# Four x tiles ahead of the K weights, four transposes on TensorE, a new order of phase 1

## Chip, cores, metric

One core of a Trainium2 chip. The metric is the device time of one execution in microseconds (us), the median over several executions. The profile's span is shorter than that time, by 1.60 to 1.80 us in the runs with the order of before (1.39 in the one with tiny transfers) and by 1.21 to 1.55 us in those with the new order; where the rest is spent is not shown. Positions below are in us from the start of the span. PE is TensorE and PEld its weight loads, DVE is VectorE, ACT ScalarE, POOL GpSimd, SP SyncE. A landing below, the end of a transfer, is the start of its issue plus the trace's time to landing, good to some 0.05 us.

## The reference

x is layer-normalized once. One branch is linear attention with 32 heads of 16, the other a gated feed-forward; both are added to x.

```python
xn = layernorm(x)                              # x: (1, 2048, 512), bf16
q, k, v = split(xn @ wqkv)                     # wqkv: (512, 1536)
pq, pk = phi(q), phi(k)                        # phi(t) = where(t > 0, t + 1, exp(t)) + 1e-6
kv, z = pk^T v per head, sum of pk
attn = ((pq kv) / (pq z + 1e-6)) @ wo
ffn = (silu(xn @ w_gate) * (xn @ w_up)) @ w_down   # 512 -> 1792 -> 512
out = x + attn + ffn
```

## The kernel before

The 2048 rows are 16 tiles of 128. Phase 1 makes, for each tile: statistics, normalization, the transposed tile, K and Q projections (four matmuls of 512 columns each), phi of both, and an accumulation of four matmuls over pk. That is 16 x 12 = 192 matmuls. Phase 2 is gate, up, down and the attention output. Programs for all engines are recorded in one list, and waits follow from what reads and writes what.

The loads stand at the head, on the SP and ACT issuers (`xhalf` is half a tile, `wpart(e, i, h)` the h-th 256 rows of the K weights, i = 1, or of the Q weights, i = 0):

```python
        xhalf("sp", 0, 0)
        xhalf("act", 0, 1)
        xload("sp", 1)
        wpart("act", 1, 0)
        wpart("sp", 1, 1)
        xload("act", 2)
        wpart("act", 0, 0)
        xload("sp", 3)
        wpart("sp", 0, 1)
        for t in range(4, 16):
            xload("sp", t)
```

Tiles 0 and 1 are only centred before their projection; their scale goes into phi. The projections rotate through four PSUM banks, which three other engines have to empty:

```python
        def nextbank():
            ring[0] += 1
            return 4 + (ring[0] - 1) % 4

        def proj(col, i, t, halves=(0, 1)):
            if 0 in halves:
                at[i, t] = nextbank()
            b = at[i, t]
            src = xcT if t in CENTRED else xnT
            for h in halves:
                K.add("pe", [(lambda e, c=c: e.matmul(
                    banks[b][:, :], src[:, c, t * P:(t + 1) * P], wqkv[:, c, col:col + D],
                    start=(c == 0), stop=(c == NDC - 1))) for c in (2 * h, 2 * h + 1)],
                    r=([("xcT", t, h)] if t in CENTRED else xkeys(t)) + [("wqkv", i, h)], w=[B(b)])

        def rest(t):
            return (1,) if t in CENTRED else (0, 1)
```

ACT takes the exponential of a bank, POOL clips it, the DVE adds the linear part from the bank and so frees it. The order of phase 1 is a text; each word is a step and a tile:

```python
        # S statistics (DVE)   R log and power (ACT)   L, P, A normalization on DVE, POOL, ACT
        # M, C centring of tile 1   a, b centring of tile 0   c, d, W, X transposes on TensorE
        # e, v, Y evacuation on ACT   f, g, w, Z evacuation on DVE   D transpose by DMA
        # K first half of a K projection, k the rest; Q, q the same for Q
        # x, m, s phi of K on ACT, POOL, DVE   y, n, u phi of Q   z keeps a Q for later
        # G accumulation over pk   J scaled tile for G (POOL)   F filler matmuls
        # r, o, N small factors per row that these steps need
        run("""
            S0 R0 b0 a0 d0 S1 M1 c0 F4 r0 C1 R1 g0 J0 W1 f0 K0 S2 r1 v1 k0 o1 S3 J1 R2 K1 x0 k1 L2 Q1 o0 x1 S4
            X2 m0 Q0 Y2 q1 m1 s0 R3 q0 R4 k2 L3 y1 s1 D3 P4 G0 S8 x2 ...   (cut)
        """)
```

## Time and profile before

| | before |
|---|---|
| time, first three executions | 212.65 us (212.52 to 213.04) |
| span of the profiled execution | 211.8 us |
| TensorE busy | 208.0 us, 98% |
| first K matmul | 5.91 us |
| first gate matmul, the start of phase 2 | 48.91 us |

Two positions matter in what follows: the start of phase 2, and in the changed kernel the start of the 13th projection matmul (the first Q matmul of tile 3). Matmul durations in a timeline overlap; work is counted in slots of 0.216 us, and what the starts show beyond that is waiting. The prediction shows how the stages are read.

### The profile page before, as it was taken

What the parts mean: (1) busy time and instruction counts of PE and PEld (TensorE: products, weight loads), DVE (VectorE), ACT (ScalarE), POOL (GpSimd) and SP (SyncE); (2) the same over time, 40 slices, a digit from 0 to 9 for tenths busy, and PEclk for the clock granted to TensorE, in tenths of its full rate; (3) what the DMA queues carried; (4) which work ended last, traced back from release to release, by engine and by line L of the source; (5) the groups of instructions that cost most, each with busy time, mean ns of one, the idle gap of its engine ahead of it and who ended that gap; (6) DMA issues with size and microseconds to landing.
All of it is one profiled execution on the core that took longest, in us unless ns stands there. A gap on an engine that the chain in (4) does not pass through costs nothing.

```text
span 211.8 us, 2736 instructions
## 1 busy us (share of the span) xinstructions
PE 208.0 (98%) x1009; PEld 95.7 (45%) x1009; DVE 129.2 (61%) x224; ACT 70.3 (33%) x146; POOL 62.9 (30%) x92
## 2 busy tenths in 40 slices
PE   8899899999999999999999999999999999999996
PEld 2344344444544444444444444444444444444455
DVE  3898988973864788654654775564639463542122
ACT  4989886406364333122131313021223122130000
POOL 3879877899402322210201220220204000000000
PEclk9999999999999999999999999999999999999999
DMA  6954731399920021102101011101011101100101
GB/s 177 353 139 101 72 73 35 63 387 370 357 88 0 3 50 25 50 0 53 25 25 25 25 29 50 25 25 50 8 44 26 50 7 46 25 25 0 49 25 53
DMA packets 27997, 16.04 MB, mean 76 GB/s; under 512 B 17872, under 2 KB 27984, under 8 KB 27984
## 3 DMA queue, kind: packets, MB, share of 16 engines
q1 hardware_dynamic: 27152, 15.15, 26.3%
q10 hardware_dynamic: 832, 0.72, 1.1%
q8 instruction: 8, 0.13, 0.3%
q14 instruction: 5, 0.04, 0.1%
HBM read 9.70 MB, written 2.10 MB: 56 GB/s over the span
## 4 chain that ended last, share of the span: by engine, by line
PE 90%; DVE 4%; DMA 3%; POOL 1%; SPq 1%; ACT 1%; issue 0%
PE pb L520 46%; PE pb L608 23%; PE pb L389 7%; PE pb L604 7%; PE pb L438 6%; DMA x_sb<-in_A_x_dram 3%; DVE pk L428 1%; SPq L178 1%; DVE pq L428 1%; DVE stats L256 1%; POOL ef L417 1%; ACT ef L410 1%; PE pb L545 0%; PE pb L598 0%; POOL xn L344 0%
## 5 line engine op out<-in xcount | busy, mean ns | idle before, releaser
L528 ACT ACTIVATE sil<-pb 128x512 bf16<-128x512 f32 x56 | 33.3, 597 | 101.2 <-PE pb L520 98.8
L533 DVE TENSOR_TENSOR hT<-pb,sil 128x512 bf16<-128x512 f32 x56 | 38.1, 687 | 36.7 <-PE pb L520 33.8
L520 PE MATMUL pb<-xnT,wg 128*128 128x512 bf16 x224 | 57.8, 379 | 0.0
L520 PE MATMUL pb<-xnT,wu 128*128 128x512 bf16 x224 | 57.8, 379 | 0.0
L608 PE MATMUL pb<-wd,hT 128*128 128x512 bf16 (+2 forms) x252 | 51.4, 355 | 0.0
L570 POOL TENSOR_TENSOR pz<-pq,zbc 128x512 f32<-128x512 bf16 x16 | 18.6, 1163 | 90.5 <-DVE den L575 78.5
L608 PEld LDWEIGHTS pb<-wd,hT 128*128 128x128 bf16 x252 | 23.5, 98 | 25.0
L520 PEld LDWEIGHTS pb<-xnT,wu 128*128 128x128 bf16 x224 | 21.9, 98 | 25.9 <-DVE hT L533 0.2
L520 PEld LDWEIGHTS pb<-xnT,wg 128*128 128x128 bf16 x224 | 21.9, 98 | 25.8
L614 DVE TENSOR_TENSOR out_sb<-pb,x_sb 128x512 bf16<-128x512 f32 (+2 forms) x18 | 11.4, 632 | 33.2 <-PE pb L608 33.2
L389 PE MATMUL pb<-wqkv,xnT 128*128 128x512 bf16 x112 | 25.2, 379 | 0.8 <-DVE pq L428 0.6
L587 DVE TENSOR_TENSOR pq<-pq,rden 128x512 bf16<-128x512 bf16 x16 | 17.5, 1094 | 0.6
L389 PEld LDWEIGHTS pb<-wqkv,xnT 128*128 128x128 bf16 x112 | 10.8, 98 | 14.5 <-DVE pq L428 1.4
L417 POOL TENSOR_SCALAR ef<-ef 128x512 bf16<-128x512 bf16 x25 | 15.8, 634 | 5.0 <-ACT ef L410 4.5
L604 PE MATMUL pb<-M,pk 128*128 128x512 bf16 (+2 forms) x72 | 16.8, 355 | 0.0
L410 ACT ACTIVATE ef<-pb 128x512 bf16<-128x512 f32 x25 | 14.7, 591 | 3.8 <-PE pb L389 3.8
L256 DVE BATCH_NORM_STATS2 stats<-x_sb 128x6 f32<-128x512 bf16 x16 | 10.9, 679 | 3.6 <-DMA x_sb<-in_A_x_dram 3.6
L438 PE MATMUL pb<-pk,xn 128*128 128x512 bf16 x56 | 12.7, 379 | 0.0
L575 DVE TENSOR_REDUCE den<-pz 128x32 f32<-128x512 f32 x16 | 10.8, 675 | 0.0
L428 DVE SCALAR_TENSOR_TENSOR pk<-pb,ef 128x512 bf16<-128x512 f32 x14 | 9.6, 685 | 1.8 <-POOL ef L417 1.6
L461 POOL TENSOR_TENSOR zacc<-zacc,pk 128x512 f32<-128x512 f32 x8 | 10.2, 1279 | 0.6
L604 PEld LDWEIGHTS pb<-M,pk 128*128 128x128 bf16 x72 | 6.8, 98 | 7.4
(77 smaller groups left out, 109.8 us busy)
## 6 DMA issues: line engine op xcount, KB each, us to landing
out_dram<-out_sb SPq DMA_DIRECT2D x15, 128.0 KB, 1.7
x_sb<-in_A_x_dram SPq DMA_DIRECT2D x14, 128.0 KB, 4.5
wg<-in_B_w_gate_dram SPq DMA_DIRECT2D x2, 896.0 KB, 8.3
wu<-in_B_w_up_dram SPq DMA_DIRECT2D x2, 896.0 KB, 9.7
wd<-in_B_w_down_dram SPq DMA_DIRECT2D x2, 896.0 KB, 13.9
wqkv<-in_A_wqkv_dram ACTq DMA_DIRECT2D x2, 256.0 KB, 4.7
wqkv<-in_A_wqkv_dram SPq DMA_DIRECT2D x2, 256.0 KB, 5.0
wqkv<-in_A_wqkv_dram SPq DMA_DIRECT2D x1, 512.0 KB, 7.8
```

Of the source, the lines that this page charges most:

```text
L389: K.add("pe", [(lambda e, c=c: e.matmul(banks[b][:, :], src[:, c, t * P:(t + 1) * P], wqkv[:, c, col:col + D], start=(c == 0), stop=(c == ...
L410: K.add("act", lambda e: e.activation(buf, banks[b][:, :], ACT.Exp), r=[B(b)], w=[bkey])
L417: K.add("pool", lambda e: e.tensor_scalar(out=buf, in0=buf, scalar1=top, scalar2=0.0, op0=ALU.min, op1=ALU.max), r=[bkey] + tkeys, w=[bkey])
L428: K.add("dve", lambda e: e.scalar_tensor_tensor(out=dst, in0=val, scalar=low, in1=mid, op0=ALU.max, op1=ALU.add), r=keys + lkeys, w=[dkey])
L438: K.add("pe", [(lambda e, c=c: e.matmul(banks[c][:, :], src[:, t, c * P:(c + 1) * P], pk[:, t, :], start=first, stop=last)) for c in range ...
L520: fns.append(lambda e, c=c, b=b, w_=w_: e.matmul(banks[b][:, :], w_[:, c, fc * P:(fc + 1) * P], xnT[:, c, C * 512:(C + 1) * 512], start=(c ...
L528: K.add("act", lambda e: e.activation(sil[:, j % 2, :], banks[gb(j)][:, :], ACT.Silu), r=[B(gb(j))], w=[("sil", j % 2)])
L533: K.add("dve", lambda e: e.tensor_tensor(out=hT[:, C % 2, fc, :], in0=banks[gb(j) + 1][:, :], in1=sil[:, j % 2, :], op=ALU.mult), r=[B(gb( ...
L570: K.add("pool", lambda e: e.tensor_tensor(out=pz[:, t % 2, :], in0=pq[:, t, :], in1=zbc[:, :], op=ALU.mult), r=[("pq", t), ("zbc",)], w=[( ...
L587: K.add("dve", lambda e: e.tensor_tensor(out=heads(pq[:, t, :]), in0=heads(pq[:, t, :]), in1=rden[:, i, :][:, :, None].broadcast_to([P, NH ...
L604: fns = [(lambda e, g=g: e.matmul(banks[bank][:, 0:hi - lo], pk[:, t, g * P:(g + 1) * P], M[:, g, lo:hi], start=(g == 0), stop=False)) for ...
L608: fns = [(lambda e, fc=fc: e.matmul(banks[bank][:, 0:hi - lo], hT[:, C % 2, fc, jj * P:(jj + 1) * P], wd[:, fc, lo:hi], start=False, stop= ...
```

## The change

Intent: have four tiles of x early, transpose them on TensorE instead of waiting for a DMA transpose, and order phase 1 so that TensorE does not wait. The loads of tiles 2 and 3 move ahead of the K weights. Tile 3 is transposed on TensorE too. `rest` lets a projection of tiles 0 to 3 run in two halves. The whole order text is new; its start is shown.

```diff
+SPLIT = (0, 1, 2, 3)
         xload("sp", 1)
+        xload("act", 2)
+        xload("sp", 3)
         wpart("act", 1, 0)
         wpart("sp", 1, 1)
-        xload("act", 2)
         wpart("act", 0, 0)
-        xload("sp", 3)
         wpart("sp", 0, 1)
         def rest(t):
-            return (1,) if t in CENTRED else (0, 1)
+            return (1,) if t in SPLIT else (0, 1)
         run("""
-            S0 R0 b0 a0 d0 S1 M1 c0 F4 r0 C1 R1 g0 J0 W1 f0 K0 S2 r1 v1 k0 o1 S3 J1 R2 K1 x0 k1 L2 Q1 o0 x1 S4
-            X2 m0 Q0 Y2 q1 m1 s0 R3 q0 R4 k2 L3 y1 s1 D3 P4 G0 S8 x2 ...   (cut)
+            S0 M1 a0 b0 c0 R0 d0 F2 C1 S3 e0 N0 W1 r0 K0 o0 f0 R3 w1 S2 K1 P3 k0 S1 R2 J0 W3 x0 k1 Q1 L2 R1 w3
+            m0 X2 q1 r1 Z2 Q3 s0 x1 o1 q3 S5 y1 K3 m1 k3 R5 n1 s1 G0 ...   (cut)
         """)
```

More of the change, by code (lines that the diff above doesn't have):

```diff
@@ L487, in bass_parallel_sum__linear_attn_block__swiglu_ffn__prompt_kernel @@
         run("""
-            S0 R0 b0 a0 d0 S1 M1 c0 F4 r0 C1 R1 g0 J0 W1 f0 K0 S2 r1 v1 k0 o1 S3 J1 R2 K1 x0 k1 L2 Q1 o0 x1 S4
-            X2 m0 Q0 Y2 q1 m1 s0 R3 q0 R4 k2 L3 y1 s1 D3 P4 G0 S8 x2 z1 m2 D4 q2 S12 R8 z0 s2 G1 P8 y0 S14 G2
-            P1 D8 y2 S15 z2 q3 n2 R12 S5 D1 k3 P12 y3 S9 R14 q4 n3 D12 x3 L14 R9 k4 u3 m3 R5 D14 N9 s3 y4 q8
-            P5 x4 S10 k8 n4 z8 D5 A9 m4 u4 G3 n1 x8 s4 D9 k12 R15 S13 m8 y8 q14 P15 x12 s8 R13 S11 q12 m12 D15
-            y14 k14 s12 n14 y12 R10 u14 n12 k5 x14 L13 R11 u12 q9 m14 D13 x5 N11 s14 k9 m5 y9 L10 A11 n8 s5
-            k15 D10 n9 S7 x9 q5 z9 m9 D11 S6 R7 G12 n0 x15 s9 R6 q13 m15 y5 L7 s15 D7 q15 n5 y13 L6 u5 n13 q10
-            y15 D6 u13 n15 k10 y10 u15 n10 k11 x10 u10 m10 k13 x11 s10 m11 k7 x13 s11 m13 k6 x7 s13 m7 q7 x6
-            s7 m6 q6 y7 L0 u8 D0 n7 q11 y6 s6 n6 G13 u7 y11 u6 n11 G5 u11 G14 u9 G11 u2 u1 G8 u0 G15 G7 G9 G10
-            G4 G6
+            S0 M1 a0 b0 c0 R0 d0 F2 C1 S3 e0 N0 W1 r0 K0 o0 f0 R3 w1 S2 K1 P3 k0 S1 R2 J0 W3 x0 k1 Q1 L2 R1 w3
+            m0 X2 q1 r1 Z2 Q3 s0 x1 o1 q3 S5 y1 K3 m1 k3 R5 n1 s1 G0 z1 L5 J1 x3 S9 K2 D5 Q0 z3 m3 S4 k2 R9 q0
+            y3 P9 s3 G1 x2 S8 R4 m2 D9 Q2 z0 q2 P4 s2 R8 k5 z2 L8 n3 D4 S15 q5 x5 y0 S12 m5 G2 D8 y5 s5 q9 y2
+            n5 S10 R15 k9 n0 y9 u5 R12 n9 k4 x9 L15 u9 D15 q4 m9 x4 L12 R10 s9 m4 q8 y4 D12 S11 P10 k8 z8 s4
+            n4 R11 D10 G9 S13 x8 N11 A11 G5 m8 u4 y8 n2 s8 D11 G3 R13 S14 A0 P13 k15 S7 R14 k12 n8 D13 x15 L14
+            S6 m15 q10 x12 D14 s15 m12 k11 y10 s12 n10 k10 D0 x11 u10 R7 m11 q15 x10 s11 q11 m10 y15 L7 R6 s10
+            D7 n15 k13 y11 u15 q13 n11 x13 L6 u11 D6 m13 q14 y13 s13 n13 q12 y14 u13 n14 k14 y12 u14 n12 q7
+            x14 u12 m14 k7 y7 L1 s14 D1 n7 k6 x7 u0 m7 q6 u7 x6 s7 m6 G4 y6 s6 n6 G12 u2 G14 u6 u1 G6 u8 G10
+            u3 G11 G15 G8 G13 G7
         """)
```

## The prediction

> **What bounds the kernel now.** I read the page first, for the share of each engine and the chain that ended last, then the table by stage, then TensorE's timeline up to 30 us, then TensorE's and the DVE's waits.
>
> ```profile
> PE 208.0 (98%) x1009; PEld 95.7 (45%) x1009; DVE 129.2 (61%) x224; ACT 70.3 (33%) x146; POOL 62.9 (30%) x92
> PE 90%; DVE 4%; DMA 3%; POOL 1%; SPq 1%; ACT 1%; issue 0%
> ```
>
> TensorE is the bound; 90% of the chain that ended last is its own work. The stages, cut where its work changes (columns: stretch, its length, busy time of each engine, clock, DMA share, GB/s):
>
> ```profile
> 0.00:5.91 5.91, 4.72 (x20) 1.79 (x21) 2.67 (x9) 3.05 (x11) 2.31 (x13) 1.00 0.66 194
> 5.91:10.18 4.27, 4.02 (x24) 1.42 (x21) 3.67 (x10) 4.01 (x15) 3.71 (x10) 1.00 1.09 356
> 10.18:25.60 15.42, 14.85 (x68) 6.60 (x69) 14.36 (x32) 14.07 (x38) 12.91 (x25) 1.00 0.61 111
> 25.60:39.41 13.81, 13.81 (x64) 6.22 (x65) 11.83 (x22) 10.13 (x21) 10.41 (x17) 1.00 0.23 48
> 39.41:48.91 9.50, 9.50 (x46) 4.31 (x45) 7.06 (x8) 0.60 (x1) 8.95 (x10) 1.00 0.93 297
> 48.91:211.80 162.89, 161.07 (x794) 75.38 (x792) 89.62 (x147) 38.46 (x64) 24.61 (x21) 1.00 0.18 50
> ```
>
> The reader should see that after 25.6 us TensorE never waits again, so only what happens before that can move the end. From 10 to 25.6 us DVE, ACT and POOL are nearly full too: they empty the PSUM banks that the projections need. TensorE's timeline (start, duration, work, wait):
>
> ```profile
> 5.68 0.40 PE L356 MATMUL pb<-ident,hT 128*128 128x128 bf16 x4 [0.33 <-DVE hT L298]
> 5.91 2.55 PE L389 MATMUL pb<-wqkv,hT 128*128 128x512 bf16 x10
> 8.30 0.39 PE L356 MATMUL pb<-ident,xn 128*128 128x128 bf16 x4
> 8.53 1.46 PE L389 MATMUL pb<-wqkv,hT 128*128 128x512 bf16 x6
> 10.18 1.04 PE L389 MATMUL pb<-wqkv,xnT 128*128 128x512 bf16 x4 [0.19 <-DVE pk L428]
> 20.55 4.48 PE L389 MATMUL pb<-wqkv,xnT 128*128 128x512 bf16 x20
> 25.60 3.61 PE L389 MATMUL pb<-wqkv,xnT 128*128 128x512 bf16 x16 [0.57 <-DVE pq L428]
> ```
>
> Durations overlap, so I count in slots. The 44 matmuls that begin at 29.91 start in 9.50 us: 0.216 us each; four transposes take 8.53 - 8.30 = 0.23. Phase 1 has 192 matmuls of 512 columns (41.45 us) and, from 5.91 on, one group of four transposes (0.23). It lasts 48.91 - 5.91 = 43.00 us, so waits take 43.00 - 41.68 = 1.32 us. Slot by slot they are 0.23 us in the first ten matmuls, 0.36 before 10.18 and 0.73 before 25.60. What they waited for:
>
> ```profile
> PEld pb L389 <- DVE pq L428: 1.4, 3, 1.0
> PEld pb L389 <- DVE pk L428: 0.9, 2, 0.7
> PEld pb L389 <- DMA wqkv<-in_A_wqkv_dram: 0.5, 1, 0.5
> DVE stats L256 <- DMA x_sb<-in_A_x_dram: 3.6, 3, 3.1
> ```
>
> The two later waits are for the DVE to free a bank; the first falls on a weight transfer. So the prize is small: no more than 1.3 us of waits, plus whatever earlier start the loads allow.
>
> **What the skill says.** "Perfetto Trace Analysis", Identifying the Most-Contended Engine, warns that matmul busy time does not tell the distance to the roofline. This trace agrees: 98% busy still holds 1.32 us of waits. "TensorE: Matmul & The Clock Gate", Back-to-back issue gap, gives about 216 ns for an isolated 512-column matmul and 131 ns for a sustained stream. The trace has 0.216 us in a sustained stream, and I use that. "DMA: Bandwidth & Descriptors", Issuing engines are not separate DMA queues, says that transfers from all issuers interleave on the same engines; the landing times below agree. "VectorE: DVE Perf Modes", The perf-mode tier table, caps copies from PSUM at 2x. The trace has 0.284 us for 256 columns and nothing for 512. At the page's 0.96 GHz and two elements a cycle, 256 more columns add 0.13, an estimate of 0.42 us.
>
> **The change, part by part.**
>
> Loads. From issue to landing, before: x0 lands near 3.1 us, x1 at 1.26 + 2.7 = 3.96; first half of the K weights 1.25 + 3.8 = 5.05; second half 1.73 + 4.5 = 6.23; x2 1.74 + 4.2 = 5.94; x3 2.19 + 4.8 = 7.0; Q halves 2.25 + 5.6 = 7.85 and 2.70 + 5.5 = 8.2. The ACT issuer's line is 5.05, 5.94, 7.85, some 0.9 us per 128 KB. Put x2 ahead of the first K half and x2 lands at 4.05, K half one at 5.96. On SP, x3 moves to about 4.9 and K half two to about 7.05. Q and x4 stay, since the bytes ahead of them are the same.
>
> Start. Before, K began at 5.91, held by transposing and evacuating x. Now x is ready first: ACT sums x1 at 4.0 rather than 4.52, and tile 0's first half is evacuated at about 5.4. K waits for its weights and starts near 6.0: **+0.09 us**.
>
> Transposes. One more tile on TensorE: **+0.23**; one DMA transpose fewer. The two dropped filler matmuls lay in idle time: 0. The DVE gets three full evacuations (1.26) and one more normalization (0.40) and loses one half evacuation (0.28), +1.4 us; ACT loses two full ones (0.58 each) and gains a half; POOL loses one normalization (0.76).
>
> Early slots, worked by hand with durations of the trace (DVE statistics 0.80 per tile from start to start, sum 0.60 to 0.66, normalization 0.32; ACT exponential 0.48, 0.67 in the centred form, log and power 0.43; POOL minimum 0.6, normalization 1.04; 0.20 from TensorE's last slot to the reader, 0.06 for other handovers):
> - K of tile 0, half one: 6.0 to 6.43. K of tile 1, half one waits for a DVE evacuation ending 6.44: starts 6.50.
> - K of tile 0, half two: weights at 7.05, so 7.10 to 7.53. Transposes of tile 3 follow at once, as POOL's normalization ends near 7.3: 7.76. Then four matmuls to 8.62, tile 2's transposes, Q of tile 1 half two, and Q of tile 3: 10.14.
> - K of tile 3 needs tile 0's bank, freed near 10.13: 10.19. Two groups end at 11.91.
> - From there I followed each bank to tile 3's accumulation at 25.7 us. The nearest calls: tile 5's K at 15.36 against its transposed data at about 14.5, and the bank for tile 9's Q, free at 17.7 against 17.95. No wait comes out.
>
> Waits in sum: 0.07 + 0.17 + 0.05 = about **0.3 us in place of 1.32: -1.05**.
>
> Tail. 104 matmuls remain at 25.7: 22.45 us, so gate and up begin at about 48.15 in place of 48.91. A bank is asked for again every four groups (3.45 us) and its chain after the matmul is 0.20 + 0.6 + 0.05 + 0.61 + 0.05 + 0.69 = 2.2 us, inside the 2.6 us of the three other groups. The last transposes are tile 1's, issued near 38, so the gate and up weights follow near 39. Before they were issued at 39.76 and 40.39 and took 5.1 and 6.9 us. They land about 44 and 46.5, ahead of 48.15. Phase 2 is unchanged at 162.9.
>
> Sum: +0.09 + 0.23 - 1.05 = about -0.75 us, or 211.9. Hand schedules forget some waits, so I give back 0.1: **212.0 us**.
>
> **Rivals.**
> 1. The K weights become the bound. For it: K half two lands some 0.8 us later and K was close to its weights. Against: much of that time goes to other work. If both halves land 0.5 us later than I say, the start moves to 6.5 and the gain is nearly gone: about 212.5.
> 2. The DVE takes the wait over. For it: 14.36 us busy of 15.42 in the stretch to 25.6, and it gets 1.4 us more, most of it before 10 us. Against: both later waits were for the order on DVE, which is changed, and it idles after 46.5. If the waits of 0.36 and 0.73 return in other places: 212.9; with 0.4 more, 213.3.
> 3. The gain is real in phase 1 but phase 2 starts on a late gate or up transfer. Against: there were over 1.5 us of slack (up landed at 47.3). This would cap the gain near 1.5 us, so it matters only if I am far too timid.
> 4. It all goes right and the start is limited by x: K at 5.6, waits of 0.1 us, 211.3.
>
> **Range and chances.** Rivals 1 and 2 set the upper end, 212.9; rival 4 the lower, 211.3. Two per cent is 4.25 us. A gain of that size would need more than all waits of phase 1 and most of the 5.9 us ahead of it, so faster is 0.01. A loss of that size would need eight waits like the longest: slower 0.01. Same: 0.98.
>
> **What would show it.** K's first slot near 6.0 and held by the weights; x2 and x3 statistics no longer waiting for DMA; the wait before 25.60 gone; the first gate matmul at 48.2 or so, with phase 2 still 162.9 us long. I am wrong if the first K slot is over 6.4, if waits of TensorE for DVE results between 10 and 26 us add to over 0.5 us, or if phase 2 changes its length.

## The result

| | before | changed |
|---|---|---|
| median | 213.16 us (6 executions, 212.52 to 213.67) | 213.15 us (6 executions, 212.86 to 213.49) |
| ratio | | 1.0004, 95% interval 0.9983 to 1.0026 |
| span of the first profile | 211.8 us | 211.7 us |
| first K matmul | 5.91 us | 6.53 us |
| 13th projection matmul | (other order) | 9.86 us |
| first gate matmul | 48.91 us | 48.77 us |

A ratio is the mean time of one kernel's fast runs over that of the other's in the same rounds, so it is not quite the ratio of the medians. The result is the same time. 213.15 us lies outside the predicted 211.3 to 212.9, and of the predicted 0.76 us by which phase 2 should start earlier the first trace has 0.14.

Half a microsecond of the miss in the absolute time is not the change's at all: the kernel before, 212.65 us in its first three executions, had a median of 213.16 over six and of 213.41 to 213.51 in the later sessions. The rest is phase 1.

The engines and the chain that ended last, on the page of the changed kernel:

```profile
PE 207.0 (98%) x992; PEld 96.1 (45%) x1011; DVE 129.4 (61%) x227; ACT 70.1 (33%) x145; POOL 61.8 (29%) x90
PE 94%; DMA 2%; issue 1%; DVE 1%; ACT 0%; POOL 0%; ACTq 0%
```

TensorE still bounds it. The DVE's part of the chain fell from 4% to 1%, that of the DMA from 3% to 2%. The stages, cut where this kernel's work changes (columns as in the prediction):

```profile
6.53:9.86 3.33, 3.33 (x20) 1.38 (x21) 3.10 (x9) 2.41 (x11) 2.55 (x5) 1.00 1.10 355
9.86:26.32 16.46, 16.35 (x75) 7.33 (x76) 16.02 (x35) 15.08 (x40) 13.22 (x26) 1.00 0.50 96
48.77:211.70 162.93, 160.29 (x779) 75.36 (x792) 89.24 (x147) 38.45 (x64) 25.52 (x22) 1.00 0.18 50
```

The 16.46 us from 9.86 to 26.32 hold 76 matmuls, 16.41 us of slots: 0.05 us of waiting, where the kernel before lost 0.73 us in the same stretch. The 22.45 us from there to the first gate matmul are as predicted, and phase 2 kept its length. So the loss must lie ahead of 9.86. TensorE's timeline there:

```profile
6.53 1.52 PE L390 MATMUL pb<-wqkv,hT 128*128 128x512 bf16 x6 [0.95 <-DMA wqkv<-in_A_wqkv_dram]
8.03 0.40 PE L357 MATMUL pb<-ident,xn 128*128 128x128 bf16 x4
...
9.20 0.40 PE L357 MATMUL pb<-ident,xn 128*128 128x128 bf16 x4
...
9.86 1.95 PE L390 MATMUL pb<-wqkv,xnT 128*128 128x512 bf16 x8
...
48.77 1.03 PE L521 MATMUL pb<-xnT,wg 128*128 128x512 bf16 x4
```

The first K matmul waited for its weights, half a microsecond longer than predicted. And the DVE, in its list of waits:

```profile
DVE stats L257 <- DMA x_sb<-in_A_x_dram: 0.7, 1, 0.7
```

It stood idle from 4.87 to 5.55 us because the new order puts tile 3's statistics first, and tile 3 landed at 5.5 rather than at 4.9.

### The profile page after: what moved, and what is told of

Read it like the earlier page. It is cut to its first block, busy times and chain, and to the rows that moved or that the text cites. A ratio compares the mean times of both kernels' runs of the same rounds, so it can differ in the third digit from the quotient of the medians.

```text
span 211.7 us, 2716 instructions
## 1 busy us (share of the span) xinstructions
PE 207.0 (98%) x992; PEld 96.1 (45%) x1011; DVE 129.4 (61%) x227; ACT 70.1 (33%) x145; POOL 61.8 (29%) x90
## 4 chain that ended last, share of the span: by engine, by line
PE 94%; DMA 2%; issue 1%; DVE 1%; ACT 0%; POOL 0%; ACTq 0%
PE pb L521 45%; PE pb L609 23%; PE pb L390 12%; PE pb L605 7%; PE pb L439 6%; DMA wqkv<-in_A_wqkv_dram 2%; PE pb L546 0%; PE pb L599 0%; DVE pq L429 0%; PE pb L357 0%; POOL ef L418 0%; ACT ef L411 0%; ACTq L179 0%; ACT L205 0%; DVE xn L327 0%
## 5 line engine op out<-in xcount | busy, mean ns | idle before, releaser
L521 PE MATMUL pb<-xnT,wu 128*128 128x512 bf16 x214 | 57.1, 379 | 0.5
L390 PE MATMUL pb<-wqkv,xnT 128*128 128x512 bf16 x110 | 25.1, 379 | 0.2
```

Of the source, the lines that this page charges most:

```text
L390: K.add("pe", [(lambda e, c=c: e.matmul(banks[b][:, :], src[:, c, t * P:(t + 1) * P], wqkv[:, c, col:col + D], start=(c == 0), stop=(c == ...
L521: fns.append(lambda e, c=c, b=b, w_=w_: e.matmul(banks[b][:, :], w_[:, c, fc * P:(fc + 1) * P], xnT[:, c, C * 512:(C + 1) * 512], start=(c ...
```

## The experiments

Two accounts were tried. **Delivery**: the order of phase 1 is as good as predicted, and what holds TensorE is the arrival of the first 1.5 MB (x0 to x3, the K and the Q weights), through the weights themselves or through tile 3 at the head of the DVE's order. **Helpers**: the chain of DVE, ACT and POOL holds TensorE whatever the loads do. A third possibility, that the first trace is an untypical one, went along with both. All runs with rounds share their rounds with the kernel before.

| run | ratio to before (95%) | first K | 13th matmul | first gate |
|---|---|---|---|---|
| before, two traces | | 5.91, 5.80 | (other order) | 48.91, 48.73 |
| changed, two traces | 0.9990 (0.9966 to 1.0015) the second time | 6.53, 6.02 | 9.86, 10.07 | 48.77, 48.98 |
| new loads, old order | 1.0017 (1.0001 to 1.0032) | 5.93 | (other order) | 49.11 |
| new order, old loads | 1.0084 (1.0039 to 1.0130) | 5.74 | 13.34 (clock lowered) | later than 50 (clock lowered) |
| tiny transfers | one look | 5.84 | (other order) | 49.14 |
| no halves for tiles 2, 3 | one look | 5.63 | 9.80 | 48.84 |
| tile 2 first | 0.9994 (0.9965 to 1.0023) | 5.80 | 9.40 | 48.73 |
| tile 2 first, first K half early | 0.9993 (0.9969 to 1.0016) | 5.56 | 9.64 | 48.55 |
| half the K and Q bytes | one look | 5.55 | 9.21 | 48.63 |
| half the bytes, tile 2 first | one look | 5.42 | 9.23 | 48.14 |
| tile 3 late, tile 10 before 11 | 0.9975 (0.9947 to 1.0003) | 6.47 | 9.51 | 48.48 |
| half the bytes, tile 10 before 11 | 0.9968 (0.9927 to 1.0009) | 5.71 | 9.22 | 48.13 |

### The loads alone

```diff
 (kernel before)
         xload("sp", 1)
+        xload("act", 2)
+        xload("sp", 3)
         wpart("act", 1, 0)
         wpart("sp", 1, 1)
-        xload("act", 2)
         wpart("act", 0, 0)
-        xload("sp", 3)
         wpart("sp", 0, 1)
```

> The kernel before with only the load order of the change (tiles 2 and 3 ahead of the K weights). Theory of the weights (the loads cost 0.6 us at the start because the K weights land later, and the new order of phase 1 gives 1.0 us of waits back): the first K matmul moves from 5.91 to about 6.5 us; the waits for the DVE before 10.18 us swallow part of it, because tile 0's bank is freed at about the same time as before, so the first gate matmul comes at about 49.1 us (48.91 in the kernel before), +0.2 us. If the delay of the weights goes through whole: 49.5, +0.6. Rival (the chain of the helper engines sets phase 1, loads are neutral): 48.9, no change.

Measured: 213.82 us against 213.43, ratio 1.0017; phase 2 starts at 49.11. TensorE's timeline of this kernel:

```profile
5.93 0.59 PE L389 MATMUL pb<-wqkv,hT 128*128 128x512 bf16 x2
7.61 1.89 PE L389 MATMUL pb<-wqkv,hT 128*128 128x512 bf16 x8 [1.09 <-DVE mv L259]
```

The 0.2 us came as expected, but not where: the first K half landed at 5.4, not 6.4, and the second at 7.5 (2.19 + 5.3), and the second group starts just after that. The label names the DVE, which had long been done; several things are waited for at once, and the landing fits. So the loads alone cost a little, and two traces with the same loads do not land them at the same times.

### The order alone

```diff
 (changed kernel)
         xload("sp", 1)
-        xload("act", 2)
-        xload("sp", 3)
         wpart("act", 1, 0)
         wpart("sp", 1, 1)
+        xload("act", 2)
         wpart("act", 0, 0)
+        xload("sp", 3)
         wpart("sp", 0, 1)
```

> The changed kernel with the load order of before. Theory of the weights in its simple form (the order is good by itself, only the loads cost): the first K matmul at 5.4 us and the first gate matmul near 48.0. Theory with the order resting on tile 3 (the order of the DVE puts tile 3's statistics ahead of the evacuations of tiles 0 and 1): tile 3 lands at 7.0 us, so K of tile 1 starts near 8.6 in place of 6.96 and the first gate matmul comes at about 50.2, +1.4 us against the changed kernel. Rival (helpers alone set phase 1): 48.8 as in the changed kernel.

Measured: 215.18 us against 213.43, ratio 1.0084. Three of its six executions had a mean clock below 1.00 (0.984, 0.992, 0.992), the profiled one among them, so its later positions are not compared, and the median and the ratio are not those of the order alone. The three at full clock have spans of 212.6 to 212.7 us, against a median of 211.7 for the kernel before in the same rounds: about 1 us more (0.6 us in mean time, 214.09 against 213.50). TensorE's timeline, then three stretches of the table by stage (TensorE's granted clock is the third number from the end):

```profile
5.74 0.60 PE L390 MATMUL pb<-wqkv,hT 128*128 128x512 bf16 x2
8.25 1.03 PE L390 MATMUL pb<-wqkv,hT 128*128 128x512 bf16 x2 [1.90 <-DVE hT L367]
```

```profile
7.00:9.00 2.00, 0.75 (x2) 0.28 (x3) 1.93 (x7) 0.50 (x2) 0.75 (x2) 0.60 1.10 353
9.00:11.00 2.00, 2.00 (x9) 1.03 (x8) 1.73 (x5) 1.32 (x4) 1.11 (x3) 0.50 1.11 349
15.00:17.00 2.00, 1.95 (x10) 0.88 (x9) 1.97 (x5) 1.95 (x5) 1.79 (x5) 1.00 0.01 2
```

The order waits for tile 3 as the second theory said: K of tile 1 started at 8.25 (8.6 expected). On top came something nobody expected: during this pause the granted clock fell to a half, at 7.38 us, 1.0 us after the last matmul had ended, and stayed there until 14.21, with matmuls 0.43 us apart. The simple form of the delivery theory, a good order held back only by its loads, falls: this order needs tile 3 early.

### Issue slots against bytes

```diff
 (kernel before; two loads of 128 bytes into a scratch tile)
         xload("sp", 1)
+        tiny("act", 0)
+        tiny("sp", 1)
         wpart("act", 1, 0)
         wpart("sp", 1, 1)
```

> The kernel before with two transfers of 128 bytes issued where the change issues tiles 2 and 3; tiles 2 and 3 stay behind their K half. It parts the issue slot from the bytes. If the issue slot delays the weights: the first K half lands at 5.05 + 0.45 = 5.5 us and the second at 6.7. If the bytes ahead of them do it: 5.1 and 6.3. In the changed kernel they land at 6.43 and 7.1.

Measured in one look: first K half at 1.82 + 3.6 = 5.42, second at 2.10 + 4.2 = 6.3. One fits the slots, the other the bytes. The two traces of the kernel before land the first half at 5.05 and 4.35, so the scatter is as large as what was to be told apart. **Inconclusive.**

### Without the halves for tiles 2 and 3

```diff
 (changed kernel)
-SPLIT = (0, 1, 2, 3)
+SPLIT = (0, 1)
-            ... Q3 s0 x1 o1 q3 S5 y1 K3 m1 k3 ... K2 D5 Q0 z3 m3 S4 k2 R9 q0 ... Q2 z0 q2 ...
+            ... q3 s0 x1 o1 S5 y1 k3 m1 ... k2 D5 Q0 z3 m3 S4 R9 q0 ... q2 z0 ...
```

> The changed kernel with the projections of tiles 2 and 3 whole again, at the place of their first half. All theories here: no difference, because both halves wait for the same transposed tile and all weights have landed by 8.3 us; the first gate matmul stays at 48.77 within 0.1 us. If the halves matter, up to 0.4 us later.

Measured in one look: first gate matmul at 48.84, 213.16 us. So the halves of tiles 2 and 3 make no difference that one look can show, as expected. This trace turned out to be worth more as another sample of the same loads. Its TensorE timeline:

```profile
5.63 1.39 PE L390 MATMUL pb<-wqkv,hT 128*128 128x512 bf16 x4
7.27 0.61 PE L390 MATMUL pb<-wqkv,hT 128*128 128x512 bf16 x2 [0.25 <-DMA wqkv<-in_A_wqkv_dram]
...
8.71 0.61 PE L390 MATMUL pb<-wqkv,hT 128*128 128x512 bf16 x2 [0.18 <-DMA wqkv<-in_A_wqkv_dram]
...
9.80 0.38 PE L390 MATMUL pb<-wqkv,xnT 128*128 128x512 bf16 x1
```

K began 0.9 us earlier than in the first trace, and the 13th matmul only 0.06 us earlier: here Q's first half was the late one (landed 8.65). A late start is therefore not the cause by itself.

### Tile 2 in tile 3's place, and with the first K half early

```diff
 (changed kernel; 2 and 3 exchanged in the whole text)
-            S0 M1 a0 b0 c0 R0 d0 F2 C1 S3 e0 N0 W1 r0 K0 o0 f0 R3 w1 S2 K1 P3 k0 S1 R2 J0 W3 ...   (cut)
+            S0 M1 a0 b0 c0 R0 d0 F2 C1 S2 e0 N0 W1 r0 K0 o0 f0 R2 w1 S3 K1 P2 k0 S1 R3 J0 W2 ...   (cut)
```

> The changed kernel with tiles 2 and 3 exchanged in the whole order of phase 1; loads as in the changed kernel. Tile 2 lands at 3.8 us, so the DVE need not stand idle from 4.87 to 5.55 us for tile 3. Theory of two equal holds (both the DVE's order behind tile 3 and the delivery of the weights bring TensorE to its 13th projection matmul at 9.8 us): the DVE's hold moves 0.7 us earlier, the weights stay (second Q half 8.2 to 8.9), so that matmul starts at 9.5 to 9.7 and the first gate matmul at 48.4 to 48.7 us (48.77 in the changed kernel): 0.1 to 0.4 us off. Theory of the weights alone (start at 6.5 passed on in full): 48.8, no change. Theory of the DVE alone: 48.1.

Measured: 213.12 us against 213.51, ratio 0.9994. The 13th matmul moved to 9.40, more than expected, but phase 2 starts at 48.73. Its loads, the same as the changed kernel's, also landed early (first K half 5.67, first Q half 7.44), so how much of the gain is the order's is not shown. TensorE's timeline shows where the 0.4 us went:

```profile
25.86 2.75 PE L390 MATMUL pb<-wqkv,xnT 128*128 128x512 bf16 x12
28.86 0.82 PE L390 MATMUL pb<-wqkv,xnT 128*128 128x512 bf16 x3 [0.25 <-DMA xnT<-xn]
```

Twelve slots end at 28.45; TensorE then waited 0.41 us for the DMA transpose of tile 11, issued at 25.5 and landed after 3.3 us in place of the usual 2.4 to 2.5. Being early, TensorE had met a new wait.

In the second version tile 2 goes to SP ahead of the second K half, and the first K half is ahead of tile 3 on ACT:

```diff
 (the kernel above)
         xload("sp", 1)
-        xload("act", 2)
-        xload("sp", 3)
+        xload("sp", 2)
         wpart("act", 1, 0)
         wpart("sp", 1, 1)
+        xload("act", 3)
         wpart("act", 0, 0)
         wpart("sp", 0, 1)
```

> As the run before it, and the load order is x0, x1, tile 2 on SP, then the second K half; on ACT the first K half before tile 3. First K half expected at 5.1 to 5.4 us, second at 6.6, tile 3 at 6.2, Q as ever at 7.7 to 8.7. Two equal holds: the first K matmul at 5.5, but Q sets the 13th matmul at 9.3 to 9.6, first gate matmul 48.2 to 48.6. Weights alone: a start 0.9 us earlier is passed on, 47.9. DVE alone: 48.1 as well.

Measured: 213.14 us against 213.51, ratio 0.9993; 13th matmul at 9.64, first gate at 48.55. The first K half landed at 4.96 and K started at 5.56, but tile 2 landed only at 5.3, and the evacuation behind it on the DVE held tile 1's K until 6.79. What the weights gained, tile 2 lost. The account of the weights alone (47.9) falls.

### Half the bytes

```diff
 (changed kernel; wrong on purpose: one row block of each half is used for both)
-            load(eng, ("wqkv", i, h), wqkv[:, 2 * h:2 * h + 2, i * D:(i + 1) * D],
-                 A_wqkv[2 * h * P:(2 * h + 2) * P, ...
+            load(eng, ("wqkv", i, h), wqkv[:, 2 * h:2 * h + 1, i * D:(i + 1) * D],
+                 A_wqkv[2 * h * P:(2 * h + 1) * P, ...
-                    ... wqkv[:, c, col:col + D],
+                    ... wqkv[:, c - c % 2, col:col + D],
```

> The changed kernel with a wrong result on purpose: of each half of the K and Q weights only the first 128 rows are loaded and used for both row blocks, so these four loads move 0.5 MB in place of 1 MB. All matmuls stay. Weights alone: the whole of phase 1 moves by about 0.9 us, first gate matmul 47.9. Two equal holds: the DVE's order behind tile 3 holds TensorE alone, 48.6 to 48.8.

> Tiles 2 and 3 exchanged and half of the K and Q bytes, wrong result on purpose. Two equal holds: both are gone, the 13th matmul starts near 9.0 and the first gate matmul comes at 47.8 to 48.1, a gain well over the sum of the gains of the two kernels that take one hold away. Weights alone: as with half the bytes in the changed order, 47.9. DVE alone: as with tiles exchanged alone, 48.1.

Their outputs are wrong, which doesn't matter for the times. The comparison with the reference does not see this fault. With half the bytes alone the 13th matmul came at 9.21, so the account of two equal holds, which had left 9.8 to the DVE, was wrong: the DVE's hold was most likely tile 3's landing, which was at 4.85 in this trace, not the DVE's own work. The first gate matmul (48.63) lies in the 48.6 to 48.8 of that account, but for another reason: TensorE again lost 0.50 us to the transpose of tile 11, which was issued at 25.1 and took 3.6 us. TensorE's timeline:

```profile
25.67 2.75 PE L390 MATMUL pb<-wqkv,xnT 128*128 128x512 bf16 x12
28.76 11.40 PE L390 MATMUL pb<-wqkv,xnT 128*128 128x512 bf16 x52 [0.34 <-DMA xnT<-xn]
```

With tile 2 first too, the 13th matmul is no earlier (9.23), there is no wait for the transpose (it was issued at 24.8 and took 2.5 us), and phase 2 starts at 48.14.

### A version meant to beat both, and both kernels again

```diff
 (changed kernel with 2 and 3 exchanged in the text)
         xload("act", 2)
-        xload("sp", 3)
         wpart("act", 1, 0)
         wpart("sp", 1, 1)
+        xload("sp", 3)
-            ... k11 y10 s12 n10 k10 D0 x11 u10 R7 m11 q15 x10 s11 q11 m10 y15 L7 R6 s10 ...
+            ... k10 y10 s12 n10 k11 D0 x10 u10 R7 m10 q15 x11 s10 q11 m11 y15 L7 R6 s11 ...
```

> A version meant to beat both: tiles 2 and 3 exchanged in the order; tile 2 stays ahead of the K weights, tile 3 goes behind them; and the K projection of tile 10 comes before that of tile 11, whose DMA transpose was waited for in two kernels. Theory (delivery of the first 1.5 MB and the DVE's order behind it hold TensorE until its 13th projection matmul, and what is gained there reaches the end unless the transpose of tile 11 takes it): 13th matmul at 9.2 to 9.5 us, no wait near 28 us, first gate matmul at 48.1 to 48.4, and 0.4 to 0.8 us less than the kernel before (ratio 0.996 to 0.998). If another hold is behind these: 48.7, ratio 0.999 to 1.000.

Measured: 212.87 us against 213.47, ratio 0.9975 (0.9947 to 1.0003); spans of 211.3 to 212.3 with a median of 211.45, against 211.8. TensorE's timeline:

```profile
6.47 1.46 PE L390 MATMUL pb<-wqkv,hT 128*128 128x512 bf16 x6 [0.61 <-DMA wqkv<-in_A_wqkv_dram]
...
9.51 2.02 PE L390 MATMUL pb<-wqkv,xnT 128*128 128x512 bf16 x8
```

No wait near 28 us, first gate at 48.48. It is probably some 0.5 us better than either kernel, but the interval includes 1. Against the kernel before, only 0.35 us of the 0.6 lie in the spans; the rest is the difference outside them that all runs of the new order have.

> The changed kernel once more, for the scatter. If the landing times differ from run to run as two kernels with the same loads suggested (first K half 6.43 and 5.34 us): the first K half lands at any time from 5.3 to 6.5, the 13th projection matmul starts at 9.6 to 9.9 all the same, the first gate matmul comes at 48.6 to 48.9, and the ratio to before is 0.998 to 1.001. If the first profile is typical: first K matmul at 6.5 again.

> The kernel before once more, a second trace for the scatter: first K matmul 5.8 to 6.0 us, first gate matmul at 48.9 to 49.2, the wait before 25.6 us there again (0.4 to 0.8 us). If its 1.32 us of waits were an outlier: 48.4 or less.

The changed kernel again: 213.32 us against 213.47, ratio 0.9990. The kernel before again, one look: 213.3 us, first gate at 48.73. TensorE's timeline of the changed kernel, and one line of that of the kernel before:

```profile
6.02 0.60 PE L390 MATMUL pb<-wqkv,hT 128*128 128x512 bf16 x2
7.04 0.60 PE L390 MATMUL pb<-wqkv,hT 128*128 128x512 bf16 x2 [0.41 <-DVE hT L367]
7.89 0.60 PE L390 MATMUL pb<-wqkv,hT 128*128 128x512 bf16 x2 [0.24 <-DMA wqkv<-in_A_wqkv_dram]
...
10.07 0.59 PE L390 MATMUL pb<-wqkv,xnT 128*128 128x512 bf16 x2
```

```profile
25.43 3.61 PE L389 MATMUL pb<-wqkv,xnT 128*128 128x512 bf16 x16 [0.59 <-DMA xnT<-xn]
```

K began at 6.02, exactly as predicted, and phase 1 still ended 0.8 us late, with both the 13th matmul and the first gate matmul later than expected for this run: this time tile 1 came late (about 4.6), its centring and evacuation behind it, then the second K half (7.8). The wait before 25.6 us of the kernel before is there again, and this time its label names a DMA transpose; the account of the prediction comes back to it.

### Delivery relieved, by halving the bytes

The last run has the changed order with tiles 2 and 3 as they were, half the bytes, and only tiles 10 and 11 exchanged as above.

> The changed kernel, its own order of tiles 2 and 3, with half of the K and Q bytes (wrong result on purpose), and tile 10's K ahead of tile 11's so that the transpose of tile 11 is not waited for. Theory of delivery (the early loads alone kept the changed kernel from the predicted time; the order of phase 1 is as good as predicted): 13th projection matmul at 9.2 to 9.3 us, no wait near 28 us, first gate matmul at 48.1 to 48.2 as the prediction had it, about 0.6 us under the kernel before. Rival (the DVE's order behind tile 3 holds as well): 13th matmul at 9.6 or later, first gate matmul 48.5 or later.

TensorE's timeline:

```profile
5.71 1.72 PE L390 MATMUL pb<-wqkv,hT 128*128 128x512 bf16 x6
7.38 0.40 PE L357 MATMUL pb<-ident,xn 128*128 128x128 bf16 x4
...
9.22 1.95 PE L390 MATMUL pb<-wqkv,xnT 128*128 128x512 bf16 x8
...
48.13 1.03 PE L521 MATMUL pb<-xnT,wg 128*128 128x512 bf16 x4
```

13th matmul at 9.22, first gate at 48.13, span 211.0, 212.73 us against 213.41. Relieved of delivery, the order with tiles 10 and 11 exchanged comes to 0.06 us of the prediction at the 13th matmul (9.28) and 0.02 us at the start of phase 2 (48.15). That it is so close is in part luck: the weights landed earlier than predicted (the last at 6.2), K began earlier, and 0.46 us of waits, behind the helpers, stand where the prediction had 0.2. Nor does the exchange explain the missing wait: tile 11 landed at 27.4 here, ahead of the 28.3 at which its K would have started in the old place. With half the bytes and no exchange it landed at 28.7, and the same 13th matmul led to 48.63. The account of the helpers (9.6 or later, 48.5 or later) falls. With four executions the ratio's interval is 0.9927 to 1.0009, so the time alone would not have shown it.

## Why the prediction was wrong

Its steps, against three traces of the changed loads and order (the run without the halves counts, as its order on TensorE is the same up to the 13th matmul), and the last run:

| | predicted | changed, first | changed, again | no halves | half bytes, tile 10 first |
|---|---|---|---|---|---|
| tile 3 landed | 4.9 | 5.5 | 5.05 | 4.7 | 4.9 |
| K half one landed | 5.96 | 6.43 | 5.65 | 5.34 | 5.03 |
| K half two landed | 7.05 | 7.1 | 7.8 | 7.2 | 5.8 |
| Q half one landed | 7.85 | 7.6 | 8.05 | 8.65 | 6.0 |
| first K matmul | 6.0 | 6.53 | 6.02 | 5.63 | 5.71 |
| waits to the 13th matmul | 0.2 | 0.28 | 1.00 | 1.12 | 0.46 |
| 13th matmul | 9.28 | 9.86 | 10.07 | 9.80 | 9.22 |
| from there to the first gate | 38.87 | 38.91 | 38.91 | 39.04 | 38.91 |
| first gate matmul | 48.15 | 48.77 | 48.98 | 48.84 | 48.13 |

(The waits are the distance from the first K to the 13th matmul, less twelve slots of 0.216 and two groups of transposes of 0.23 us. Predicted 9.28 is 10.14 less the four slots of tile 3's Q.)

- **What failed first: the step "Loads", and with it the early part of "waits in sum about 0.3 us".** The prediction took landing times from one trace, moved them along by 0.9 us per 128 KB of one issuer's line, and then treated them as certain. In three traces of the same loads they scatter by 0.8 us for tile 3, 1.1 us for the first K half and 1.05 us for the first Q half, and not together: in these three, the earlier the first K half, the later the first Q half (in the run with tile 2 first both were early). TensorE needs all of them in turn, so what counts is the latest each time. Start and waits trade against each other (6.53 with 0.28, 5.63 with 1.12), and the 13th matmul comes 0.5 to 0.8 us after the predicted 9.28 in all three. The Trainium skill says that all issuers' transfers share the same engines ("DMA: Bandwidth & Descriptors", Issuing engines are not separate DMA queues), and the prediction quoted it and then calculated each issuer's line by itself; a DMA busy share of 1.10 from 6.53 to 9.86 us in the first trace fits the page. In three runs with half the bytes the 13th matmul came at 9.21 to 9.23: that delivery held TensorE until then is shown. A sign of being wrong that the prediction had named, a first K slot after 6.4, came in the first trace (6.53) and not in the other two. How the engines divided their time between the two issuers' lines, and why it differs from run to run, stays open; the run with tiny transfers did not tell.
- **The order's part came out in size, but not for the reason given.** The prediction read the 0.73 us before 25.60 as a wait for the DVE to free a bank, from the profile's label. But that matmul is the Q projection of tile 9; the DVE had freed its bank by 24.54 (it is the one that Q of tile 14 had used), and tile 9's DMA transpose, which took 5.1 us, landed at 25.46. In the second trace the label names the transpose, which landed at 25.29, ahead of a start at 25.43. The new order issues it at 14.9 in place of 20.4 us. The wait is gone in every trace of the new order at full clock, and the stretch from the 13th matmul to phase 2 takes 38.91 to 39.04 us in the table, against a predicted 38.87.
- **A second hold was overlooked.** The prediction followed the order only to 25.7 us and let 104 matmuls run from there without a wait. Two traces in which TensorE was early (13th matmul at 9.21 and 9.40) waited 0.50 and 0.41 us for the transpose of tile 11. So loads on time would not by themselves have been sure to give 48.15. In the three traces of the changed loads and order that transpose landed at 27.85 to 28.15 us, in time. Why it took 3.3 and 3.6 us in those two and 2.4 to 2.5 in the others is open.
- **Smaller terms.** One more group of transposes costs 0.23 us as said. The evacuation of a whole tile on the DVE, an estimate of 0.42 us, measured 0.41 and 0.42.
- **Rival 1 was the nearest**: it named late weights and about 212.5 us. It missed that tile 1 or tile 3 would do the same damage through the DVE.
- **Rival 2, the DVE as a new bound by its own work, did not come**: in the last run it has no hold on TensorE after the 13th matmul. Its normalization of tile 2 took 0.65 us beside POOL's work in place of 0.40, which the hand schedule had left out.
- **The absolute level was a second error**, 0.5 us and nothing to do with the change: three executions gave 212.65, and the range was laid around that. In the same rounds the kernel before had 213.16.
- "Same" at 0.98 was right. The sum has slips that change nothing: 0.3 in place of 1.32 is -1.02, not -1.05, and the terms as written add to -0.73, not -0.75.

In short: the new order saves TensorE the 0.73 us of waiting after 10 us; ahead of that, late arrivals and the extra transposes put its 17th projection matmul at 10.66 to 10.93 us (four slots after the 13th), where the kernel before had 10.18 and 9.99. The two cancel.

## What to carry to other kernels

Where a chain needs several transfers in turn, don't add up their mean landing times: take several traces of the same kernel, and plan for the latest of them, because that is what the engine behind waits for. Halving the bytes on purpose, with all the arithmetic kept, is a cheap way to ask whether delivery or order is the bound. And a wait taken away early in a kernel pays only if the engine, arriving early, finds nothing new to wait for: two runs here lost 0.4 to 0.5 us of it at a DMA transpose 19 us later.

## What the Trainium skill lacked or had wrong

- "DMA: Bandwidth & Descriptors", Anatomy of one DMA, models a transfer (one issued from GpSimd) as a fixed time plus its bytes. It has no word on how far the landing of the same transfer in the same program differs between executions: for the first K half 5.05 and 4.35 us in two traces of the kernel before, 6.43 and 5.65 in two of the changed one.
- The same page, Latency and other measured facts, gives a bandwidth for DMA transposes (261 GB/s) and no time for one tile; "VectorE: DVE Perf Modes" has one for 128x128 alone. A 128x512 bf16 tile here mostly took 2.4 to 2.6 us from issue to landing, and at times up to 5.1 us.
- "TensorE: Matmul & The Clock Gate", Back-to-back issue gap, gives 131 ns per 512-column matmul in a sustained stream with weight loads. All runs here show 0.216 us at full clock (44 matmuls start in 9.50 us), which is what the section gives for an isolated one.
- The same page, What's actually happening, puts the return to half clock after an idle window of about 3.4 us. In the run with the new order and the old loads the clock was full from 3.97 us and fell to a half at 7.38, after a stretch of that length in which TensorE was busy for 56% of the time and paused for no more than the last 1.0 us at once. Three of that run's six executions showed a lowered mean clock; only one was profiled.
